# Batch 0 of an attention and MLP kernel: x by halves on two engines, the mean as one column, other fills for the matrix engine

## The chip, the cores and the metric

The kernel runs on one core of a Trainium2 chip. The metric is device time in microseconds (us). A core has a matrix engine (PE, whose weight loads are listed apart as PEld), a vector engine (DVE), a scalar engine for activations (ACT), a general one (POOL) and a queue engine for transfers (SP). Each takes its instructions in the order of the program and waits on semaphores that the others raise.

## The reference

For each of 8 batches and 8 heads, with 576 tokens of 64 dimensions, a linear attention is computed; its output, heads side by side, is a token's x of 512 numbers. Then a layer norm and an MLP with a residual follow:

```python
q_s = softmax(q, axis=-1)            # over the 64 dimensions of a head
k_s = softmax(k, axis=2)             # over the 576 tokens
kv  = einsum('bhsd,bhse->bhde', k_s, v)
x   = einsum('bhsd,bhde->bhse', q_s, kv)   # then (batch, token, 512)
xn  = (x - mean(x)) / sqrt(var(x) + 1e-6) * g_ln
out = x + maximum(xn @ w_ch1, 0) @ w_ch2   # 512 -> 2048 -> 512
```

## The kernel before, in words

Tokens are worked on in chunks: chunks 0 to 7 are the first 512 tokens of each batch, as 4 tiles of 128; chunk 8 gathers the remaining 64 tokens of each batch. For every chunk a list of MLP steps on PE (`mlp_steps`) is written out, and side work (the attention of a later chunk, weight sums, loads) is placed into it at given positions by `run`. Nothing is reordered: the schedule is manual, so the order of the calls is the order on each engine.

The change lies in the start, `first_batch`, and in what it calls. There all loads are issued, and batch 0 is brought to the point where its MLP can begin:

- `warm` issues matmuls on a tile of zeros (`junk`) that nothing reads; 17 stand at the start, 6 between the transposes of the first two token tiles.
- `exp_qt(0, t)` is the exponential of q for token tile t, on ACT; `norm_q` divides by the sum, on DVE; `eq_pT` transposes the result on PE (`ptr`) and copies it into `eqT`, on the engine named. Tiles 0 and 1 are normalized before the transpose, tiles 2 and 3 not.
- `exp_k0` and `z0_mm` give the exponential of k and its sums; `kv0_mm(j)` makes k'v for a pair of heads j in 6 matmuls, and one DVE instruction (line 322) scales it, keeps the two diagonal blocks and adds up each row (`kvbox["sum"]`). From this sum comes `mbc[:, j]`, a 128x128 tile in which each row holds minus the row's sum over 512. On ACT (line 327) for j = 0 to 2, on DVE (line 331) for j = 3.
- `xT_mm(j, kh)` builds x minus its mean for token tiles 0 and 1, already transposed, in PSUM (`pxT`): for each half kh of the 512 features one bank of two 128-blocks, with the kv product where the pair j belongs to the half, and with two products by `mbc[:, j]` that take the mean away. `xT_out(i)` evicts block i, times g, into `xnT`: blocks 0 and 1 on DVE (line 351), 2 and 3 on ACT (line 353).

Then `mlp_steps(0)` begins: four column blocks of w1 times the first feature half of tiles 0 and 1 (`ph`, line 520, w1 taken from `w1_raw`, whose first 512 columns come in two transfers, one for each half of the features). In between, at position 2 of `run`, z, po, x (`x_fast`, line 464) and xn (`x_normed`, line 475) of token tile 2; at 4 z and po of tile 3; then the second feature half; at 6 the transposes of tile 2's xn (`xn_pT`, line 928) and x of tile 3. The loads of v, q tiles 2 and 3, w1 and w2 are issued in this order by POOL, after a small copy (`gate`, line 1004) that waits for q tiles 0 and 1.

Of the kernel before, what the change touches and what calls it, by code (L numbers as in the profile page):

```python
# [12 lines left out]
FP32 = mybir.dt.float32  # L13
BF16 = mybir.dt.bfloat16
AF = mybir.ActivationFunctionType
# [5 lines left out]
def kernel(  # L21
# [16 lines left out]
    nc = tc.nc  # L38

    B, H, S, D = q.shape  # L40
    DM = H * D
    DH = 4 * DM
    P = 128
    T = 4
# [4 lines left out]
    NP = H // 2  # L49
# [10 lines left out]
    const = ctx.enter_context(tc.tile_pool(name="const", bufs=1))  # L60
# [12 lines left out]
    eps_ln = const.tile([P, 1], FP32)  # L73
    gate = const.tile([P, 4], FP32)
    ones = const.tile([P, 1], BF16)
    junk = const.tile([P, P], BF16)
    scrap = const.tile([P, 512], BF16)
    bones = const.tile([P, 2], BF16)
    ones_w = const.tile([P, P], BF16)
    diag = const.tile([P, P], FP32)  # L80
    mbc = const.tile([P, NP, P], BF16)
    g_one = const.tile([P, KO1], FP32)
    w1_sb = wts.tile([P, KO1, DH], BF16, name="w1_raw")
    w1g = const.tile([P, KO1, DH], BF16)
# [12 lines left out]
    def load_w1(nb):  # L97
        cols = slice(nb * 512, nb * 512 + 512)
        nc.gpsimd.dma_start(w1_sb[:, :, cols], w1_src[:, :, cols])
# [100 lines left out]
    def new_eq(c):  # L200
        eqs[c] = (
            att.tile([P, T, H, D], BF16, tag="eq", name="eq", bufs=1),
            sml.tile([P, T, H], FP32, tag="zq", name="zq"),
            sml.tile([P, T, H], FP32, tag="rq", name="rq"),
        )
        eqTs[c] = att.tile([P, T, NP, P], BF16, tag="eqT", name="eqT")
# [10 lines left out]
    def exp_qt(b, t):  # L217
        if t == 0 and b:
            new_eq(b)
        nc.scalar.activation(eqs[b][0][:, t], raws[b][2][:, :, t], AF.Exp)  # L220
# [66 lines left out]
    kvbox = {}  # L287
# [9 lines left out]
    def k0_mm(j, t):  # L297
        hs = slice(2 * j, 2 * j + 2)
        return eks[0][0:P0, t, hs, :], raws["v0"][0:P0, hs, t, :], P
# [16 lines left out]
    def kv0_mm(j):  # L316
        pool, tag = (att_ps, "a") if j < 2 else (mm_ps, "m")
        pkv = pool.tile([P, P], FP32, tag=tag, name="pkv")
        for t in range(T0):
            lhsT, rhs, w = k0_mm(j, t)  # L320
            nc.tensor.matmul(pkv[:, 0:w], lhsT, rhs, start=(t == 0), stop=(t == T0 - 1))
        nc.vector.scalar_tensor_tensor(
            kv_sb[:, 0, j, :], in0=pkv, scalar=kvbox["rz"][:, j : j + 1], in1=diag,
            op0=ALU.mult, op1=ALU.mult, accum_out=kvbox["sum"][:, j : j + 1],
        )
        if j < NP - 1:
            nc.scalar.activation(
                mbc[:, j], ones_w, AF.Copy, scale=kvbox["sum"][:, j : j + 1]
            )
        else:  # L330
            nc.vector.tensor_scalar_mul(
                out=mbc[:, j], in0=ones_w, scalar1=kvbox["sum"][:, j : j + 1]
            )

    def xT_mm(j, kh):

        if j == 0:
            pobox["T", kh] = mm_ps.tile([P, 2, 2, P], FP32, tag="m", name="pxT")
        ops = [(kv_sb[:, 0, j, :], j % 2)] if j // 2 == kh else []
        ops += [(mbc[:, j], i) for i in range(2)]  # L340
        for n, (lhsT, i) in enumerate(ops):
            nc.tensor.matmul(
                pobox["T", kh][:, i], lhsT, eqTs[0][:, 0:2, j, :],
                start=(j == 0 and n == 0), stop=(j == NP - 1 and n >= len(ops) - 2),
                skip_group_check=True,
            )

    def xT_out(i):
        dst, src = xnTs[0][:, 0:2, i, :], pobox["T", i // 2][:, i % 2]
        if i < 2:  # L350
            nc.vector.tensor_scalar_mul(out=dst, in0=src, scalar1=g_one[:, i : i + 1])
        else:
            nc.scalar.activation(dst, src, AF.Copy, scale=g_one[:, i : i + 1])
# [506 lines left out]
        for _, fn in side[done:]:  # L860
            fn()

    def warm(n):

        w = mm_ps.tile([P, 4, P], FP32, tag="m", name="warm")
        for _ in range(n):
            nc.tensor.matmul(w, junk, junk[:, 0:4].to_broadcast([P, 4, P]), start=True, stop=True)

    def prep_fast(b):

# [54 lines left out]
    def pe_T(dst, src, t, eng, scale=None):  # L925
        ptr = mm_ps.tile([P, NP, 2 * P], BF16, tag="m", name="ptr")
        for j in range(NP):
            nc.tensor.transpose(ptr[:, j, 0:P], src[:, j * P : j * P + P], ident)  # L928
        if eng is nc.scalar:
            nc.scalar.copy(dst[:, t], ptr[:, :, 0:P])  # L930
        elif scale is not None:
            nc.vector.tensor_mul(dst[:, t], ptr[:, :, 0:P], scale.to_broadcast([P, NP, P]))
        else:
            nc.vector.tensor_copy(out=dst[:, t], in_=ptr[:, :, 0:P])
# [10 lines left out]
    def eq_pT(c, t, eng):  # L945
        pe_T(eqTs[c], eqs[c][0][:, t].rearrange("p h d -> p (h d)"), t, eng)
# [10 lines left out]
    def first_batch():  # L957

        nc.scalar.preload_act_table_set("natural_log_exp_and_others")
        raws[0] = (  # L960
            mlp.tile([P, H, T0, D], FP32, tag="hT", name="kt0", bufs=1), None,
            raw.tile([P, H, T, D], FP32, tag="qt", name="qt"),
        )
        k0, _, q0 = raws[0]
        v0 = mlp.tile([P, H, T0, D], BF16, tag="hs", name="v0", bufs=1)
        raws["v0"] = v0

        def load_q0(t, tn, eng):
            ts = slice(t, t + tn)
            eng.dma_start(  # L970
                q0[:, :, ts],
                q[0, :, 0:SM, :].rearrange("h (p t) d -> p h t d", t=T)[:, :, ts],
            )

        def src0(x, h0, hn):
            return x[0, h0 : h0 + hn].rearrange("h (p t) d -> p h (t d)", t=T0)

        load_q0(0, 2, nc.sync)
        for h0 in range(0, H, 2):
            nc.sync.dma_start(  # L980
                k0[0:P0, h0 : h0 + 2].rearrange("p h t d -> p h (t d)"), src0(k, h0, 2)
            )
        raws["g"] = outp.tile([KO1, P], FP32, tag="ot", name="g_rows")
        nc.scalar.dma_start(
            raws["g"], bass.AP(moe_g_ln.tensor, moe_g_ln.offset, [[P, KO1], [1, P]])
        )
        nc.vector.memset(junk, 0.0)
        nc.vector.memset(eps_ln, 1e-6)
        nc.vector.memset(ones, 1.0)
        nc.vector.memset(bones, 0.0)  # L990
        nc.vector.memset(bones[0:64, 0:1], 1.0)
        nc.vector.memset(bones[64:P, 1:2], 1.0)
        nc.vector.memset(ones_w, -1.0 / DM)
        nc.vector.memset(diag, 0.0)
        for ps in halves:
            nc.vector.memset(diag[ps, ps], 1.0)
        nc.vector.memset(kv_sb[:, 1:B], 0.0)
        nc.vector.memset(vr, 0.0)
        for half in range(2):
            nc.vector.memset(vr[64 * half : 64 * half + 64, :, 4 * half : 4 * half + 4, D:], 1.0)  # L1000
        nc.vector.memset(vm[:, :, :, :, D:], 1.0)
        make_identity(nc, ident)
        nc.gpsimd.tensor_copy(out=ident_f, in_=ident[0:KO1, 0:KO1])
        nc.gpsimd.tensor_copy(out=gate, in_=q0[:, 1, 0, 0:4])
        for h0, hn in ((0, 4), (4, 2), (6, 2)):
            nc.gpsimd.dma_start(  # L1006
                v0[0:P0, h0 : h0 + hn].rearrange("p h t d -> p h (t d)"), src0(v, h0, hn)
            )
        for t in range(2, T):
            load_q0(t, 1, nc.gpsimd)  # L1010
        for kh in range(2):
            ks = slice(2 * kh, 2 * kh + 2)
            nc.gpsimd.dma_start(w1_sb[:, ks, 0:512], w1_src[:, ks, 0:512])
        for nb in range(1, 4):
            load_w1(nb)
        load_w2(0)
        load_w2(1)

        new_eq(0)
        start_x(0)  # L1020
        warm(17)
        for t in range(2):
            exp_qt(0, t)
            norm_q(0, t)
        eq_pT(0, 0, nc.vector)
        warm(6)
        eq_pT(0, 1, nc.vector)
        for j in range(NP):
            exp_k0(j)
            z0_mm(j)  # L1030
            if j == NP - 2:
                g_columns()
        recip_z()
        kv0_mm(0)
        kv0_mm(1)
        kv0_mm(2)
        xT_mm(0, 0)
        kv0_mm(3)
        exp_qt(0, 2)
        exp_qt(0, 3)  # L1040
        xT_mm(1, 0)
        xT_mm(2, 0)
        xT_mm(0, 1)
        xT_mm(3, 0)
        xT_out(0)
        xT_out(1)
        eq_pT(0, 2, nc.scalar)
        xT_mm(1, 1)
        xT_mm(2, 1)
        eq_pT(0, 3, nc.vector)  # L1050
        xT_mm(3, 1)
        xT_out(2)
        xT_out(3)

    def q0_rest(t):
        z_q(0, t)
        for i in range(NP):
            po_mm(0, t, i)
# [132 lines left out]
```

## Time and profile before

| what | value |
|---|---|
| time, median of 3 runs | 262.56 us (262.25 to 262.58) |
| the profiled execution | 262.09 us, span 260.3 us |
| PE busy | 98% of the span |
| DVE, ACT, POOL busy | 86%, 68%, 40% |
| transfers | 45.04 MB, 173 GB/s on the mean |
| PE idle for want of a w1 block, once, at 16.7 us | 0.4 us |

Times in the profile count from the start of the span. A line of the timeline gives the start and length of a group of instructions, its engine, line and operation, what it writes and reads, how many there are, and in brackets how long the engine had been idle before and which engine or transfer ended that. A matmul's length has its latency in it; how fast PE takes work is seen better from the distance of the weight loads.

### The profile page before, as it was taken

How to read it: one execution, taken by the hardware profiler on the slowest of the kernel's cores; microseconds unless marked ns; L12 is line 12 of the kernel's file. 1: busy time of each engine (PE TensorE's matmuls, PEld its weight loads, DVE VectorE, ACT ScalarE, POOL GpSimd, SP SyncE). 2: the span in 40 equal slices, each digit the busy share in tenths (PEclk: the TensorE clock that was granted, in tenths of full speed). 3: DMA queues.
4: the chain of work that ended last, by engine and by line, in shares of the span. 5: the costliest groups of instructions: out<-in, count | busy, mean ns of one | idle time of the engine just before them, and what ended most of it. 6: DMA issues, size and time to landing. Idle time of an engine off the chain costs nothing.

```text
span 260.3 us, 7286 instructions
## 1 busy us (share of the span) xinstructions
PE 253.9 (98%) x2885; PEld 215.6 (83%) x2885; DVE 223.1 (86%) x542; ACT 177.5 (68%) x348; POOL 103.2 (40%) x160
## 2 busy tenths in 40 slices
PE   8899999999999999999999999999999999999993
PEld 3689755788888888888888988888889888888883
DVE  6768996989989998899889988998899889957873
ACT  4747790997988685888588858885788386647400
POOL 3953247410299409800980098008200900190000
PEclk9999999999999999999999999999999999999999
DMA  6999999988699995999699859989902630422014
GB/s 198 257 203 208 354 221 332 257 169 308 118 122 321 268 120 107 300 247 107 142 300 235 86 135 304 232 89 161 279 0 50 142 137 1 77 71 99 3 40 121
DMA packets 82618, 45.04 MB, mean 173 GB/s; under 512 B 58196, under 2 KB 79192, under 8 KB 82584
## 3 DMA queue, kind: packets, MB, share of 16 engines
q0 software_dynamic: 32464, 21.76, 45.8%
q1 hardware_dynamic: 49488, 22.29, 36.8%
q10 hardware_dynamic: 632, 0.53, 0.7%
q8 instruction: 22, 0.36, 0.6%
q14 instruction: 12, 0.10, 0.1%
HBM read 36.70 MB, written 9.44 MB: 177 GB/s over the span
## 4 chain that ended last, share of the span: by engine, by line
PE 92%; DMA 4%; POOL 2%; DVE 0%; issue 0%
PE ba L604 21%; PE bx L762 20%; PE bb L762 10%; PE ph L520 8%; PE bb L604 6%; PE be L604 5%; PE bc L604 5%; PE pc L556 5%; PE bc L762 5%; DMA w_raw<-in_moe_w_ch_dram 3%; PE pkv L371 2%; DMA qt<-in_q_dram 2%; PE po L403 2%; PE ptr L928 1%; PE po L414 1%; POOL v L1006 1%
## 5 line engine op out<-in xcount | busy, mean ns | idle before, releaser
L604 PEld LDWEIGHTS <-hs 128*128 128x128 bf16 x512 | 49.6, 98 | 6.0
L269 POOL TENSOR_TENSOR tq<-xnT 128x256 bf16<-128x256 bf16 x30 | 20.1, 671 | 85.3 <-PE bc L604 73.9
L762 PEld LDWEIGHTS <-w_raw 128*128 128x128 bf16 x480 | 46.7, 98 | 5.5
L604 PEld LDWEIGHTS <-hT 128*128 128x128 bf16 x392 | 37.6, 98 | 4.2
L762 PEld LDWEIGHTS <-w1g 128*128 128x128 bf16 x360 | 34.7, 98 | 4.3 <-issue 0.2
L762 PE MATMUL bx<-tq,w_raw 128*128 128x256 bf16 x240 | 31.3, 273 | 0.0
L604 PE MATMUL ba<-w_q,hs 128*128 128x256 bf16 x256 | 30.6, 273 | 0.0
L786 ACT COPY bc<-bx 128x512 f32<-128x512 f32 x30 | 16.7, 596 | 19.1 <-PE bx L762 19.1
L427 ACT ACTIVATE scrap<-x,mv 128x512 bf16<-128x512 bf16 x32 | 23.1, 723 | 4.6 <-DVE mv L457 4.4
L793 DVE TENSOR_TENSOR bb<-bx,s 128x512 f32<-128x512 f32 x30 | 19.5, 694 | 7.2 <-ACT s L790 4.5
L804 ACT ACTIVATE hT<-bb 128x512 bf16<-128x512 f32 x30 | 16.3, 595 | 9.3 <-PE bb L762 9.3
L804 ACT ACTIVATE hT<-bc 128x512 bf16<-128x512 f32 x30 | 16.5, 595 | 8.5 <-PE bc L762 8.5
L796 DVE TENSOR_TENSOR hT<-bx,s 128x512 bf16<-128x512 f32 x30 | 19.3, 684 | 3.2 <-PE bx L762 3.1
L587 DVE TENSOR_TENSOR hs<-hT 128x1024 bf16<-128x1024 bf16 x32 | 21.4, 672 | 0.5 <-ACT hT L804 0.5
L229 DVE TENSOR_REDUCE zq<-eq 128x16 f32<-128x1024 bf16 (+1 forms) x20 | 20.7, 1049 | 0.5 <-ACT eq L220 0.5
L269 POOL TENSOR_TENSOR tq<-xnT,tq 128x256 bf16<-128x256 bf16 x30 | 20.0, 669 | 1.1
L449 DVE SCALAR_TENSOR_TENSOR x<-po,rq 128x256 bf16<-128x256 f32 x48 | 17.5, 420 | 1.7 <-PE po L403 1.7
L790 ACT COPY s<-bb 128x512 f32<-128x512 f32 x30 | 16.6, 622 | 0.0
L804 ACT ACTIVATE hT<-bx 128x512 bf16<-128x512 f32 x30 | 16.4, 610 | 0.0
L762 PE MATMUL bx<-xnT,w1g 128*128 128x256 bf16 x120 | 16.2, 273 | 0.0
L762 PE MATMUL bx<-tq,w1g 128*128 128x256 bf16 x120 | 15.9, 272 | 0.0
L762 PE MATMUL bc<-xnT,w1g 128*128 128x256 bf16 x120 | 15.8, 273 | 0.0
(157 smaller groups left out, 535.0 us busy)
## 6 DMA issues: line engine op xcount, KB each, us to landing
out_dram<-ot POOLq DMA_DIRECT2D x30, 256.0 KB, 4.4
kt<-in_k_dram SPq DMA_DIRECT2D x5, 1024.0 KB, 11.6
qt<-in_q_dram SPq DMA_DIRECT2D x4, 1024.0 KB, 9.9
qt<-in_q_dram POOLq DMA_DIRECT2D x2, 1024.0 KB, 12.7
kt<-in_k_dram POOLq DMA_DIRECT2D x2, 1024.0 KB, 14.5
vm<-in_v_dram POOLq DMA_DIRECT2D x16, 128.0 KB, 12.4
qt<-in_q_dram SPq DMA_DIRECT2D x3, 512.0 KB, 5.7
w_raw<-in_moe_w_ch_dram POOLq DMA_DIRECT2D x3, 512.0 KB, 10.5
```

The source lines that it names most:

```text
L229: nc.vector.reduce_sum(eqs[c][1][:, ts], eqs[c][0][:, ts], axis=AX.X)
L269: nc.gpsimd.tensor_tensor(out=dst[:, t], in0=x[:, t], in1=y[:, t], op=ALU.subtract)
L427: nc.scalar.activation(scrap, x[:, t], AF.Square, bias=mv[:, t, 0:1], scale=-float(DM), accum_out=mv[:, t, 1:2],)
L449: nc.vector.scalar_tensor_tensor(x[:, t].rearrange("p (i two d) -> p i two d", two=2, d=D)[:, :, half], in0=pobox[c, t][half], scalar=1.0, ...
L520: nc.tensor.matmul(ph[:, m % 2, at : at + tn], (w1g if c else w1_sb)[:, ko, m * P : (m + 1) * P], xnTs[c][:, t0 : t0 + tn, ko, :], start=( ...
L587: nc.vector.tensor_tensor(out=dst, in0=x, in1=y, op=op)
L604: nc.tensor.matmul(hbox[bank][:, t, cs], lhsT, rhs[:, cs], start=first and (own or t == 0) and k == 0, stop=k == KH - 1, skip_group_check= ...
L762: nc.tensor.matmul(dst[:, q], lhsT, rhs, start=first and q == 0 and ko == 0, stop=ko == 1, skip_group_check=True)
L786: nc.scalar.copy(at[g, "c"], at[g, "x"])
L793: nc.vector.tensor_tensor(out=at[g, "b"], in0=at[g, "x"], in1=at[g, "s"], op=ALU.add)
L796: nc.vector.tensor_tensor(out=h_out(g, 1, 1), in0=at[g, "x"], in1=at[g, "s"], op=ALU.add)
L804: nc.scalar.activation(h_out(g, odd, half), at[g, name], AF.Relu)
```

## The change

Four things change, all in the start of batch 0.

1. `mbc` and the tile of constants `ones_w` go. In their place is `kvm`, one column for each pair j: the row's sum times -1/512. `xT_mm` gives the matrix engine this column as a 128x128 weight tile, read 128 times with step 0.
2. `xT_out`: blocks 0 and 2 go to DVE, 1 and 3 to ACT.
3. The order. Before, the products of x with the second half stood between those of the first, and the transposes of token tiles 2 and 3 among them, the copy of tile 2 on ACT and of tile 3 on DVE; both `exp_qt(0, 2)` and `exp_qt(0, 3)` stood ahead of them. Now the first half is finished and evicted, then comes `exp_qt(0, 3)`, the second half and its eviction, and then the transposes of tiles 2 and 3, with both copies on DVE. As before, `xT_mm(0, 0)` stands ahead of the last kv product.
4. The fills: `junk` is a float32 tile, with a bf16 one (`junk_h`) beside it. In place of 17 bf16 fills there are 4 float32 ones, in place of 6 there are one float32 and two bf16.

```diff
-    junk = const.tile([P, P], BF16)
+    junk = const.tile([P, P], FP32)
+    junk_h = const.tile([P, P], BF16)
-    ones_w = const.tile([P, P], BF16)
-    mbc = const.tile([P, NP, P], BF16)
+    kvm = const.tile([P, NP], BF16)
...
+        total = kvbox["sum"][:, j : j + 1]
         if j < NP - 1:
-            nc.scalar.activation(
-                mbc[:, j], ones_w, AF.Copy, scale=kvbox["sum"][:, j : j + 1]
-            )
+            nc.scalar.activation(kvm[:, j : j + 1], total, AF.Copy, scale=-1.0 / DM)
         else:
-            nc.vector.tensor_scalar_mul(
-                out=mbc[:, j], in0=ones_w, scalar1=kvbox["sum"][:, j : j + 1]
-            )
+            nc.vector.tensor_scalar_mul(out=kvm[:, j : j + 1], in0=total, scalar1=-1.0 / DM)
...
-        ops += [(mbc[:, j], i) for i in range(2)]
+        ops += [(kvm[:, j : j + 1].to_broadcast([P, P]), i) for i in range(2)]
...
-        if i < 2:
+        if i % 2 == 0:
             nc.vector.tensor_scalar_mul(out=dst, in0=src, scalar1=g_one[:, i : i + 1])
...
-    def warm(n):
+    def warm(n, src=junk):
...
-            nc.tensor.matmul(w, junk, junk[:, 0:4].to_broadcast([P, 4, P]), start=True, stop=True)
+            nc.tensor.matmul(w, src, src[:, 0:4].to_broadcast([P, 4, P]), start=True, stop=True)
...
         nc.vector.memset(junk, 0.0)
+        nc.vector.memset(junk_h, 0.0)
...
-        nc.vector.memset(ones_w, -1.0 / DM)
...
-        warm(17)
+        warm(4)
...
-        warm(6)
+        warm(1)
+        warm(2, junk_h)
...
-        kv0_mm(0)
-        kv0_mm(1)
-        kv0_mm(2)
+        for j in range(NP - 1):
+            kv0_mm(j)
         xT_mm(0, 0)
-        kv0_mm(3)
+        kv0_mm(NP - 1)
         exp_qt(0, 2)
-        exp_qt(0, 3)
-        xT_mm(1, 0)
-        xT_mm(2, 0)
-        xT_mm(0, 1)
-        xT_mm(3, 0)
+        for j in range(1, NP):
+            xT_mm(j, 0)
         xT_out(0)
         xT_out(1)
-        eq_pT(0, 2, nc.scalar)
-        xT_mm(1, 1)
-        xT_mm(2, 1)
-        eq_pT(0, 3, nc.vector)
-        xT_mm(3, 1)
+        exp_qt(0, 3)
+        for j in range(NP):
+            xT_mm(j, 1)
         xT_out(2)
         xT_out(3)
+        for t in range(2, T):
+            eq_pT(0, t, nc.vector)
```

## The prediction

> **What bounds the kernel now.** I read four views, from the whole to the place of the change. First the page's engine line, which says that the matrix engine is the bound on average:
>
> ```profile
> PE 253.9 (98%) x2885; PEld 215.6 (83%) x2885; DVE 223.1 (86%) x542; ACT 177.5 (68%) x348; POOL 103.2 (40%) x160
> ```
>
> Then the chain that ended last, in order of time (start, length, what):
>
> ```profile
> 0.74 4.29 DMA qt<-in_q_dram
> ...
> 9.82 6.86 DMA w_raw<-in_moe_w_ch_dram
> 16.68 0.05 issue
> 16.72 0.61 PE ph L520 x4
> ...
> 19.74 11.37 PE ph L520 x112
> 31.11 2.37 PE pc L556 x11
> ```
>
> Up to 16.72 us the chain is transfers: q, the descriptors behind it on POOL, then the second 256 KB block of w1. From 16.72 on it is PE without a hole. So what the change does ahead of 16.72 counts only where it makes PE or its feeders miss that point; behind it, a delay goes one to one to the end. The waits of PE over the whole run say the same, for besides the first instruction there are only these:
>
> ```profile
> PE ptr L928 <- DVE eq L923: 1.0, 1, 1.0
> PE ph L520 <- DMA w_raw<-in_moe_w_ch_dram: 0.4, 1, 0.4
> ```
>
> Last the timeline of the place itself (start, length, engine, line, in brackets the idle time before):
>
> ```profile
> 11.14 1.17 ACT L327 ACTIVATE mbc<-ones_w,kvs 128x128 bf16<-128x128 bf16 x3 [1.16 <-DVE kv_sb L322]
> ...
> 12.44 1.40 ACT L220 ACTIVATE eq<-qt 128x512 bf16<-128x512 f32 x2
> ...
> 12.77 0.25 DVE L331 TENSOR_SCALAR mbc<-ones_w,kvs 128x128 bf16<-128x128 bf16 x1
> 13.07 0.11 PEld L342 LDWEIGHTS <-mbc 128*128 128x128 bf16 x2 [0.26 <-DVE mbc L331]
> ...
> 13.51 0.88 DVE L351 TENSOR_SCALAR xnT<-pxT,g_one 128x256 bf16<-128x256 f32 x2 [0.49 <-PE pxT L342]
> ...
> 14.52 0.42 PEld L520 LDWEIGHTS <-w_raw 128*128 128x128 bf16 x4
> ...
> 15.90 0.23 PEld L414 LDWEIGHTS <-eqT 128*128 128x128 bf16 x4
> ...
> 16.40 0.35 DVE L475 TENSOR_SCALAR xn<-x,st 128x512 bf16<-128x512 bf16 x1
> ...
> 16.72 0.33 PEld L520 LDWEIGHTS <-w_raw 128*128 128x128 bf16 x4 [0.59 <-DMA w_raw<-in_moe_w_ch_dram]
> ...
> 17.06 0.32 PEld L928 LDWEIGHTS <-xn 128*128 128x128 bf16 x4
> ```
>
> The reader is to see two slacks. The last weight load ahead of the w1 wait ends at 16.13, so PE's queue could run 0.59 us later for nothing. The transpose of xn for token tile 2 is loaded at 17.06, and its source is done at 16.40 + 0.35 = 16.75; with the 0.05 us from a DVE end to a load (13.02 to 13.07) that chain has 0.26 us.
>
> **The change, part by part.** The profiled execution took 262.09 us (span 260.3, 1.8 around it), 0.47 under the median of the runs, 262.56. I add differences in the profile to the median.
>
> *Fills.* PE now begins with 4 float32 fills for 17 bf16 ones, and has 1 float32 and 2 bf16 for 6.
>
> ```profile
> 3.96 0.15 PEld L867 LDWEIGHTS <-junk 128*128 128x128 bf16 x1 [0.28 <-issue]
> ...
> 4.31 1.62 PEld L867 LDWEIGHTS <-junk 128*128 128x128 bf16 x8 [0.20 <-issue]
> ...
> 9.73 0.29 PEld L953 LDWEIGHTS gcp<-ident_f,g_rows 4*128 4x128 f32 x2
> ```
>
> The loads come every 0.43 us up to 3.96 and every 0.21 us after 4.31: PE runs at half pace for its first 3.3 us. The one float32 product shows as two loads and two matmuls, so a float32 fill costs at least two bf16 fills, and at most four if the doubled bytes also halve the pace of each; I take four, the dearer. [...] From 1.05 (the float32 memset is 0.165 as for diag, 0.112 before) two fills take 1.71 each and two 0.85 each: they end near 6.2, where the 17 ended at 6.42. PE then waits for DVE's normalized eq until 7.41 in both. The second group is 0.85 + 2 x 0.21 = 1.28 against 6 x 0.21 = 1.28, plus a float32 load of 0.18 in place of 0.10: 0.07 later at the second transpose. On DVE the memsets add 0.05 + 0.11 and remove 0.165 (ones_w): nothing.
>
> *Mean as one column.* Four 128x128 writes become 128x1. ACT: three of 0.40 become 0.21 (nearest row the 128x4 rstd at 0.206; bounds 0.08, DVE's accumulator read of one column, and 0.40, no gain). DVE: 0.254 becomes 0.14 (row L1124, 128x1; bounds 0.08 and 0.254). The first column is ready 0.19 earlier, so the last kv product could start at 11.64 in place of 11.83. But the third v block was issued at 6.7 and lands 5.0 later, at 11.7; I take 11.75. So the fourth kv step on DVE starts at 12.29 (12.37), its column is ready at 12.83 (13.02), and x's bank is complete for eviction at 13.32 (13.51): 0.19 gained. That 0.08 of gain at the v block also swallows the 0.07 of the fills. The 16 weight loads now read a column with step 0; mbc's take 98 ns at a pitch of 107. The fills read their moving side with step 0 at full pace, so I take 98; the dear bound is 182, the float32 load.
>
> *The evictions.* xT_out(1) goes from DVE to ACT. In the compiled order of the changed kernel that ACT instruction waits for a DVE semaphore which xT_out(0) sets; both read one PSUM tile. So they run one behind the other: DVE 13.32 to 13.80 (0.478), ACT 13.83 to 14.30 (0.470), against 14.39 before: 0.09 gained, not 0.4. [...]
>
> *What is queued behind that wait.* On ACT it is exp_qt(0, 3), which ran from 13.21 to 13.84. It now starts at 14.20 (two such ACT evictions had a pitch of 0.37, 14.83 to 15.67 for two) and ends at 14.83. PE holds its order: the transposes of token tile 3 now stand ahead of x's first products with w1, and both wait. Transposes at 14.88, and 0.27 later (13.97 to 14.24 before) the first w1 load at 15.15, against 14.52: 0.63 later, although x itself was ready earlier. The transposes of tile 2 and the other half of x (ten matmuls at 0.107) fit into the hole at 13.1 to 14.88. The two eqT copies, both on DVE now (0.42 each), end near 15.8, ahead of z for tile 3 near 16.3. xT_out(3) on ACT, behind the late exp, ends near 15.3; the products of the second half stand near 16.7. Both are covered, by 0.5 and 1.4 us. SP and POOL issue the same transfers in the same order, so w1 lands when it did.
>
> *Sum.* PE reaches the w1 wait at 16.13 + 0.63 = 16.76: only 0.04 over. But z, po, x_fast and xn of tile 2 also move by 0.63, so xn ends at 17.38 and its transposes load at 17.43 against 17.06: **0.37 us later**. From there the DVE and PE steps to tile 3 (19.34) are a tight chain, and PE is dense to the end. Forecast: 262.56 + 0.37 = 262.93, say **262.95 us**, slower by a breath. Its own range: without the v wait and with the short columns 0.17 less, 262.75; with columns as dear as before (0.08 + 0.11), no overlap on ACT (0.10) and the fills' 0.07 uncovered, 263.3.
>
> **The rivals.**
>
> *1. The fills leave PE at half pace* (slower). Place: the load pitch at 4 us. If 4 float32 fills do not lift the pace at 4.3, they last to 1.05 + 4 x 1.71 = 7.9, past 7.41: 0.5 later at the first transposes, which all passes on, since DVE, ACT and PE to xn of tile 2 form one chain; with 0.37 that is 263.4. If the pace stays low to the w1 wait, some 3 us of PE work (24 products of 0.06, 20 of 0.107) doubles besides: about 265. It decides once half pace lasts past 6. For it: a third of the fills' instructions, and 1.2 us idle behind them. Against: by the dearer price PE is busy as long as before. [...]
>
> *2. The one-column loads are slow* (slower). At 182 ns each of 16 loads costs 0.075 more than the pitch: 0.6 ahead of xT_out(0), with 0.1 covered by the wait for the fourth column: 262.95 + 0.5 = 263.5. Against: step 0 runs at full pace on the moving side.
>
> *3. The delay is swallowed, or the two evictions do overlap* (not slower). If ACT's eviction ran from 13.32, exp_qt(0, 3) would end at 14.32 and the first w1 load come at 14.64: 0.12 late, under both slacks, so 262.56. It decides where exp_qt(0, 3) ends before 14.45. Against: the semaphore.
>
> *4. Faster.* The w1 landing is not moved, and in before nothing between 16.72 and the end waits for anything the change touches. Only what no row shows (other PSUM banks and SBUF addresses, a different phase of the pace) could give it: 262.0.
>
> **How the numbers follow.** A difference of 0.2%, 0.53 us, is about what a measurement of this kernel can tell from none. Forecast 0.57; of its own range a good third lies past 263.08, so 0.22 slower and 0.35 same. Rival 1: 0.15 and rival 2: 0.08, slower. Rival 3: 0.10, same. Rival 4: 0.10, faster. Together: faster 0.10, same 0.45, slower 0.45. The range leaves out half of rival 4 and the dear half of rival 1: 262.3 to 264.2.
>
> **What would show it.** In the profile of the changed kernel: xT_out(1) on ACT starting after xT_out(0) on DVE has ended; exp_qt(0, 3) behind it, ending near 14.8; a new wait of PE transposes on ACT of some 0.5 us; the w1 wait nearly gone; the transposes of xn for tile 2 near 17.4. Right on the fills: loads or matmuls at full pace by 4.5. I am wrong if PE still waits 0.4 us for w1, if the step-0 loads take over 0.11, or if fills run into 7.4.

## The result, and the profile after

| what | value |
|---|---|
| kernel before, median of 6 runs beside the changed one | 262.49 us (262.0 to 262.76) |
| changed kernel, median of 6 runs | 263.84 us (263.69 to 264.9) |
| ratio, with its 95% interval | 1.0061 (1.0042 to 1.0081) |
| profiled execution of the changed kernel | 264.3 us, span 262.5 us |

The change makes the kernel 1.35 us slower. I had forecast a loss of 0.37 us. The profiled execution lies 0.46 us above the median, so its details are read with that in mind. From here on "before" and "after" are the two kernels, and a kernel that I made is called by what it changes.

The page of after has PE still nearly full, with eleven fewer instructions:

```profile
PE 255.6 (97%) x2874; PEld 215.8 (82%) x2874; DVE 223.8 (85%) x543; ACT 176.3 (67%) x347; POOL 103.3 (39%) x160
```

The waits of PE in after, besides its first instruction (engine, tile and line, what it waited for: us in total, times, longest):

```profile
PE z L306 <- ACT ek L293: 0.5, 1, 0.5
PE ptr L925 <- DVE eq L920: 0.4, 1, 0.4
PE bb L759 <- DVE hT L526: 0.4, 1, 0.4
PE ptr L925 <- ACT eq L220: 0.3, 1, 0.3
```

The wait for w1 is gone, as forecast, and the transposes of tile 3 wait for ACT's exponential, as forecast. But the first line is new and lies, in time, ahead of all that the new order touches: PE waits for the last exponential of k. The chain that ended last, from its beginning (start, length, what), leads to the same place:

```profile
2.85 7.33 DMA kt<-in_k_dram
10.18 0.02 issue
10.20 0.85 ACT ek L293
11.06 0.05 issue
11.10 0.30 PE z L306 x6
```

In before the chain began with q and went through w1, and k stood nowhere in it. The timeline of after shows how the delay travels (start, length, engine and line, what; in brackets the idle time before):

```profile
5.41 1.15 ACT L220 ACTIVATE eq<-qt 128x512 bf16<-128x512 f32 x2 [3.39 <-DMA qt<-in_q_dram]
...
10.20 0.84 ACT L293 ACTIVATE ek<-kt 96x768 bf16<-96x768 f32 x1 [0.30 <-DMA kt<-in_k_dram]
...
14.37 0.48 DVE L348 TENSOR_SCALAR xnT<-pxT,g_one 128x256 bf16<-128x256 f32 x1 [0.49 <-PE pxT L339]
...
14.88 0.47 ACT L350 ACTIVATE xnT<-pxT,g_one 128x256 bf16<-128x256 f32 x1 [0.32 <-DVE xnT L348]
...
15.26 0.62 ACT L220 ACTIVATE eq<-qt 128x512 bf16<-128x512 f32 x1
...
16.11 0.37 PEld L517 LDWEIGHTS <-w_raw 128*128 128x128 bf16 x4
...
18.42 0.23 PEld L925 LDWEIGHTS <-xn 128*128 128x128 bf16 x4 [0.41 <-DVE xn L472]
```

The point on which the forecast turned, the transposes of xn for tile 2, comes at 18.42 in place of 17.06: 1.36 us later, which is the loss of the medians. But xT_out(0) already starts at 14.37 in place of 13.51, although each step that the change touches ahead of it became shorter or stayed. So 0.86 of the 1.36 is there before the new order has done anything. (In this execution another 0.8 us is lost behind 18.42, in two waits, near 34.8 and 58.8 us; of the kernels below with late transfers some have both, some only the first and one has neither, and I draw nothing from them.)

What is late is transfers. The answer on transfers for the first 12 us, before (bytes and mean rate; for the queue q1 its packets, their MB and the time they took as a share of what the 16 DMA engines have; then for each kind of transfer its size and the median us from issue to landing):

```profile
DMA packets 2816, 2.73 MB, mean 227 GB/s; under 512 B 147, under 2 KB 2711, under 8 KB 2816
...
q1 hardware_dynamic: 1872, 1.70, 50.6%
...
kt<-in_k_dram SPq DMA_DIRECT2D x4, 288.0 KB, 5.5
...
qt<-in_q_dram POOLq DMA_DIRECT2D x2, 256.0 KB, 5.0
w_raw<-in_moe_w_ch_dram POOLq DMA_DIRECT2D x2, 256.0 KB, 6.1
```

and the same of after:

```profile
DMA packets 2719, 2.42 MB, mean 201 GB/s; under 512 B 130, under 2 KB 2689, under 8 KB 2719
...
q1 hardware_dynamic: 1872, 1.70, 58.4%
...
kt<-in_k_dram SPq DMA_DIRECT2D x4, 288.0 KB, 6.3
...
qt<-in_q_dram POOLq DMA_DIRECT2D x2, 256.0 KB, 6.3
w_raw<-in_moe_w_ch_dram POOLq DMA_DIRECT2D x2, 256.0 KB, 6.7
```

The same transfers, of the same size, in the same order on the same queues, move 11% less in the same time. They are not cut into more packets: the queue q1 moves 1872 packets with 1.70 MB both times, and these packets take longer, 58.4% of the engines' time in place of 50.6%. The edit to the calls cannot do that: it touches no transfer. So the experiments had two questions: which part of the change slows transfers that it does not name, and what is left of the loss once they run as before.

### The profile page after: what moved, and what is told of

Its sections match the earlier page's. It is cut to its first block, busy times and chain, and to the rows that moved or that the text cites. A ratio compares the mean times of both kernels' runs of the same rounds, so it can differ in the third digit from the quotient of the medians.

```text
span 262.5 us, 7264 instructions
## 1 busy us (share of the span) xinstructions
PE 255.6 (97%) x2874; PEld 215.8 (82%) x2874; DVE 223.8 (85%) x543; ACT 176.3 (67%) x347; POOL 103.3 (39%) x160
## 4 chain that ended last, share of the span: by engine, by line
PE 77%; DMA 15%; POOL 2%; DVE 2%; issue 1%; SPq 1%; ACT 1%; POOLq 0%
PE ba L601 21%; PE bx L759 20%; PE bb L759 10%; DMA w_sb<-in_moe_w_ch_dram 8%; PE bb L601 6%; PE be L601 5%; PE bc L601 5%; PE bc L759 5%; DMA vr<-in_v_dram 4%; DMA kt<-in_k_dram 3%; PE pkv L368 2%; PE po L400 2%; PE pxT L339 1%; POOL kt L130 1%; DVE w_q L567 1%
## 5 line engine op out<-in xcount | busy, mean ns | idle before, releaser
L759 PE MATMUL bb<-tq,w_raw 128*128 128x256 bf16 x120 | 15.7, 272 | 0.4 <-DVE hT L526 0.4
```

Of the source, the lines that this page charges most:

```text
L759: nc.tensor.matmul(dst[:, q], lhsT, rhs, start=first and q == 0 and ko == 0, stop=ko == 1, skip_group_check=True)
```

## The experiments

Every kernel here computes the whole result, and each ratio is to the kernel before, run beside it on the same chip (262.30 us in the first group of runs, 262.29 in the second, 262.58 in the third, whose chip gave wider intervals).

**First group: the parts, one by one.** The column alone: `mbc` and `ones_w` out, `kvm` in, with the old fills, evictions and order of calls.

```diff
-    ones_w = const.tile([P, P], BF16)
     diag = const.tile([P, P], FP32)
-    mbc = const.tile([P, NP, P], BF16)
+    kvm = const.tile([P, NP], BF16)
...
-        ops += [(mbc[:, j], i) for i in range(2)]
+        ops += [(kvm[:, j : j + 1].to_broadcast([P, P]), i) for i in range(2)]
```

> Before with the mean as one column and nothing else. Step-0 weight loads at full pace: 98 ns each at a pitch of 107 ns, x's first bank complete 0.1 to 0.2 us earlier, the time the same as before to 0.2 us, since the w1 wait takes up the gain. Slow loads would show as 0.15 us and more each, and 0.3 us or more on the time.

Measured: 263.58 us, ratio 1.0052 (1.0035 to 1.0069). A part that saves work on ACT and DVE brings nearly the whole loss. The timeline of this kernel shows where:

```profile
10.51 0.84 ACT L292 ACTIVATE ek<-kt 96x768 bf16<-96x768 f32 x1 [0.40 <-DMA kt<-in_k_dram]
...
15.32 0.63 ACT L219 ACTIVATE eq<-qt 128x512 bf16<-128x512 f32 x1 [0.46 <-DMA qt<-in_q_dram]
```

The last exponential of k starts at 10.51, against 9.1 in before, and that of q tile 3 waits for its transfer until 15.32, though in this kernel it still stands ahead of the evictions. Both waits end with a transfer.

The column with the new fills added:

```diff
-    junk = const.tile([P, P], BF16)
+    junk = const.tile([P, P], FP32)
+    junk_h = const.tile([P, P], BF16)
...
-        warm(17)
+        warm(4)
...
-        warm(6)
+        warm(1)
+        warm(2, junk_h)
```

> The old order and the old evictions, with the one-column mean and the float32 fills. If the time is lost to the order (exp_qt(0, 3) and the transposes of tile 3 late), this is within 0.3 us of before. If it is lost to the fills (half pace held to about 6.5 us, or q and k landing later beside them), it is slower by most of the 1.35 us that the full change lost, that is by 0.8 us or more, and its profile shows k's last block on ACT near 10 us and not near 9.1.

Measured: 263.72 us, 1.005 (1.0033 to 1.0068): 0.14 us over the column alone, well inside both intervals. The fills are not where the time went. (The new fills were not tried on before alone.)

The whole change with the old fills:

```diff
-        warm(4)
+        warm(17)
...
-        warm(1)
-        warm(2, junk_h)
+        warm(6)
```

> The full change but with the 17 and 6 bf16 fills. If the order loses the time, it stays slower than before by 0.4 to 1.35 us. If the fills lose it, it is within 0.4 us of before. Pace: loads of the fills every 0.21 us from about 4.3 us on, as in before.

Measured: 263.24 us, 1.0041 (1.0024 to 1.0058). The interval overlaps that of after, and q tiles 2 and 3 are late here too (5.9 us to landing). The two pairs put the new fills at 0.14 us and at 0.41 (1.35 less 0.94), neither of it clear of the intervals.

The new order of calls alone, on before (the block from `kv0_mm` on, as in the change; evictions and `mbc` as before):

```diff
-        exp_qt(0, 3)
-        xT_mm(1, 0)
-        xT_mm(2, 0)
-        xT_mm(0, 1)
-        xT_mm(3, 0)
+        for j in range(1, NP):
+            xT_mm(j, 0)
         xT_out(0)
         xT_out(1)
-        eq_pT(0, 2, nc.scalar)
...
+        exp_qt(0, 3)
...
+        for t in range(2, T):
+            eq_pT(0, t, nc.vector)
```

> Before with the new order of calls and nothing else (old fills, mbc, both first evictions on DVE). exp_qt(0, 3) then waits behind nothing on ACT but exp_qt(0, 2), so the transposes of tile 3 stand only behind x's second half: if the late exp behind the eviction is the loss, this is within 0.2 us of before; if the transposes standing ahead of the first w1 products are the loss by themselves, it is slower by 0.3 us or more.

Measured: 262.72 us, 1.0011 (1.0 to 1.0022), 0.42 us in the medians; the interval begins at nothing. Transfers land as in before (q tiles 2 and 3 in 5.2 us). So the order costs about what I had given it. But it did not lose it in the way I had described, as this kernel's chain shows:

```profile
12.81 0.69 DVE mbc L331
13.50 0.05 issue
13.55 1.48 PE pxT L342 x12
15.03 0.24 PE ptr L928 x4
15.27 0.03 issue
15.29 0.76 DVE eqT L934 x2
```

With both evictions on DVE, `exp_qt(0, 3)` isn't late here: it ends at 13.88, against 13.84 before. What is late is the column on DVE (0.69 long in place of 0.25), and with it xT_out(0), by 0.47 us. The transposes of xn for tile 2 are late by 0.46, no more:

```profile
13.98 0.88 DVE L351 TENSOR_SCALAR xnT<-pxT,g_one 128x256 bf16<-128x256 f32 x2 [0.49 <-PE pxT L342]
...
17.52 0.23 PEld L928 LDWEIGHTS <-xn 128*128 128x128 bf16 x4 [0.34 <-DVE xn L475]
```

From the one to the other it takes 3.54 us, as in before (3.55, from 13.51 to 17.06), where 0.26 of it was slack. So the new order has a second price, near 0.25 us: the transposes stand behind the second half of x, and their two copies, both on DVE now, stand ahead of the reciprocal that x of tile 2 needs. In this execution that price went into the slack, and the longer column alone accounts for the loss. Why the column took longer isn't known, so the 0.42 us can't be put down to the new queueing.

**Second group: addresses.** What the column part changes for a transfer is where its target lies. In the compiled programs the tiles of SBUF follow each other. `mbc` and `ones_w` take 1280 bytes of each partition, `kvm` 8, for which 32 are set aside; so every tile behind it moves by 1248 bytes. In before the tiles of q, k and the first w1 start at multiples of 256 bytes. With the column alone, and in after, they start 32 bytes past such a multiple. The theory: this is the cause, and neither the step-0 loads nor the column itself. The plainest test takes before, changes no instruction of the work and adds a tile that nothing reads (with a memset of one element):

```diff
     mbc = const.tile([P, NP, P], BF16)
+    pad = const.tile([P, 16], BF16)
...
+        nc.vector.memset(pad[0:1, 0:1], 0.0)
```

> Before with one unused tile of 32 bytes per partition behind mbc, and no other change in what is computed or in which order. If the start address is the cause, 1.0 to 1.4 us slower than before, with q landing near 5.4 and k's last block after 9.9 us. If not, within 0.2 us of before.

Measured: 263.61 us, 1.0062 (1.0039 to 1.0085). Thirty-two bytes that nobody uses cost 1.32 us, as much as the whole change. Its transfers in the first 12 us and its chain:

```profile
DMA packets 2719, 2.41 MB, mean 201 GB/s; under 512 B 130, under 2 KB 2691, under 8 KB 2719
...
qt<-in_q_dram POOLq DMA_DIRECT2D x2, 256.0 KB, 6.3
w_raw<-in_moe_w_ch_dram POOLq DMA_DIRECT2D x2, 256.0 KB, 6.7
```

```profile
8.52 6.37 DMA qt<-in_q_dram
14.89 0.02 issue
14.91 0.64 ACT eq L221
15.55 0.05 issue
15.60 0.40 PE ptr L929 x4
```

These are after's figures, 201 GB/s, 6.3 and 6.7, out of a program that has before's work to the instruction. The unused tile moves the operands of the engines as well as the targets of transfers. But the first transfer of q, issued at 0.74 us, when no engine works on these tiles yet, already takes 4.6 us here, in place of the 4.3 in before, so the transfers themselves are slower.

The counter-test keeps the column and gives its tile 256 bytes, so that all behind it starts at multiples of 256 again:

```diff
-    kvm = const.tile([P, NP], BF16)
+    kvm = const.tile([P, P], BF16)
```

> As the run before, padded to 256 bytes, so that the targets keep before's address modulo 256 as well. If a multiple of 64 is enough, it is as fast as with 64 bytes; if 256 counts, this one is at 262.3 and the one with 64 bytes is slower by 0.4 us or more.

Measured: 262.26 us, 1.0001 (0.9989 to 1.0014). The loss of the column is gone to the last tenth, and its transfers are before's:

```profile
DMA packets 2813, 2.71 MB, mean 226 GB/s; under 512 B 147, under 2 KB 2711, under 8 KB 2813
...
qt<-in_q_dram POOLq DMA_DIRECT2D x2, 256.0 KB, 5.0
```

The same with 64 bytes (`const.tile([P, 32], BF16)`):

> Before with the one-column mean alone, but the column's tile padded from 8 to 64 bytes per partition, so that q, k, v and w1 start at a multiple of 64 bytes again as in before; nothing else differs from the run with the column alone, which lost 1.28 us. If the loss is the start address of the transfers' targets, this is within 0.3 us of before and k's last block reaches ACT near 9.2 us. If the column itself loses it (the weight loads, the missing memset), it stays at 263.3 or more and k's last block comes after 10 us.

Measured: 263.43 us, 1.0044 (1.0031 to 1.0057), q tiles 6.2 us to landing. A start at a multiple of 64 is not enough.

The whole change with its column tile at 256 bytes, the same one-line edit:

> The full change with the column's tile padded to 256 bytes. If the address explains all but the order, what is left is the late exp_qt(0, 3) behind the eviction on DVE, by the prediction 0.37 us: 262.5 to 262.9. If address and order do not add up, as slow as the full change, 263.6 or more.

Measured: 262.63 us, 1.0015 (1.0006 to 1.0024). This is the forecast's own case, with the transfers as in before: +0.34 us against the forecast's 0.37. Its chain through the place:

```profile
13.61 0.50 DVE xnT L348
14.11 0.02 issue
14.13 0.47 ACT xnT L350
14.61 0.53 ACT eq L220
15.13 0.05 issue
15.18 0.40 PE ptr L925 x4
...
17.19 0.37 DVE xn L472
17.55 0.05 issue
17.60 0.40 PE ptr L925 x4
```

**Third group: what is left.** The last 0.34 us: the late exponential, or the rest of the order? The whole change with aligned tiles, and `exp_qt(0, 3)` back ahead of the evictions:

```diff
+        exp_qt(0, 3)
         xT_out(0)
         xT_out(1)
-        exp_qt(0, 3)
```

> The full change with the column's tile padded to 256 bytes, and exp_qt(0, 3) moved ahead of xT_out(0). If the exponential queued behind the eviction on ACT is what the change itself costs, this is back at 262.3, within 0.15 us of before, with the transposes of tile 3 loaded before 14.6 us. If the transposes standing ahead of the first w1 products are enough by themselves, it stays at 262.6 or so, as with the padding alone.

Measured: 262.77 us, 0.9998 (0.9978 to 1.0018). The interval holds both nothing and the 0.34 us, so the time settles nothing. In the trace the exponential is early, ending at 13.29, and from xT_out(0) to the transposes of xn it takes 3.72 us (13.11 to 16.83), where the kernel just above took 3.99 and before 3.55. Of before's 3.55 us 0.26 was slack. Some of the price goes with the exponential, some stays, as far as one execution of each can show it.

The whole change with aligned tiles and the old order of calls:

```diff
+        exp_qt(0, 3)
+        xT_mm(1, 0)
+        xT_mm(2, 0)
+        xT_mm(0, 1)
+        xT_mm(3, 0)
...
+        eq_pT(0, 2, nc.scalar)
...
```

> All of the change but the new order of calls, padded to 256 bytes: one-column mean, evictions of each half on DVE and ACT, float32 fills. If only the order costs anything once the addresses are as in before, 262.3, within 0.15 us of before. If the fills or the evictions cost something beside it, 262.5 or more.

Measured: 262.36 us, 0.9992 (0.9963 to 1.0021), and 3.30 us for that stage. Column, split evictions and new fills together lose nothing that can be told from before, and gain nothing either.

The column alone with a tile of 128 bytes (`const.tile([P, 64], BF16)`):

> Before with the column alone, its tile padded to 128 bytes: q, k, v and w1 start at a multiple of 128 and not of 256 bytes. If 256 is what counts, as slow as with 64 bytes, 263.2 to 263.6; if 128 is enough, 262.3.

Measured: 263.13 us, 1.0029 (1.0006 to 1.0051), q tiles 5.9 us. A multiple of 128 doesn't do either, by the time and by the q tiles. The loss in the medians, 0.55 us, is smaller, and k takes 5.8 us to landing here (median), next to the 5.1 to 6.0 of the seven kernels with aligned tiles. Whether 128 is milder than 32 isn't settled: the five kernels at 32 past a multiple of 256 gave 5.9 to 6.5 us for the q tiles, and the intervals of the times overlap.

The column at 256 bytes, and small tiles and two unused ones made wide enough that the targets of w2 and of the later v tiles start at multiples of 256 as well (in before w2's starts 96 bytes past one):

```diff
-    g_one = const.tile([P, KO1], FP32)
+    g_one_w = const.tile([P, 64], FP32)
+    g_one = g_one_w[:, 0:KO1]
...
+    pad_a = const.tile([P, 112], BF16)
     vm = const.tile([P, 2, T, H, VW], BF16)
+    pad_b = const.tile([P, 64], BF16)
```

> Before with the column padded to 256 bytes, and with small pads that also bring w2, the rest tiles of v and the v tiles of later batches to a multiple of 256 bytes. If a start off 256 bytes slows any transfer into SBUF, the w2 loads land earlier than in before; the time moves little, since PE waits for no transfer after 16.7 us: 262.0 to 262.3. A time above 262.5 would speak against the address as the cause.

Measured: 262.46 us, 0.9993 (0.9972 to 1.0013), and w2 lands in 16.0 us as in before. Nothing is to be had there: no version beat before by more than its interval.

## Why the prediction was right or wrong

Sign and range were right, the place and most of the size were not. The forecast was 262.95 us, the result 263.84; of the loss of 1.35 us the forecast had 0.37. That the result lies inside the range is luck: the upper part of the range stood for slow fills and slow column loads (rivals 1 and 2), and neither of them cost time.

*The step that failed* is the sentence that closes the part on the queued work: "SP and POOL issue the same transfers in the same order, so w1 lands when it did." The first half is true, and the second doesn't follow. The loads of the first 15 us land later, since their targets moved by an amount that isn't a multiple of 256 bytes. Among those are k, whose last exponential starts at 10.20 in place of 9.1, and q tiles 2 and 3. I had the thought in the wrong rival: SBUF addresses stand under "Faster", as something "no row shows", with 0.10. They belonged on both sides, and the addresses could have been read from the compiled program without a run. Shown by: before with 32 unused bytes has the loss, the column with 256 bytes has none.

For 256 stand the q tiles 2 and 3 of the four kernels that differ in the column's tile alone: 6.5, 6.2 and 5.9 us to landing with 32, 64 and 128 bytes set aside for it, 5.0 with 256. By what mechanism the start of the written side slows a transfer no run shows.

*The step that held* is the sum for the order: 0.37 us forecast, 0.34 with aligned tiles (262.63 against 262.29, ratio 1.0015, 1.0006 to 1.0024, that is 0.16 to 0.63 us). In that kernel the second eviction starts on ACT 0.02 after the first has ended on DVE (14.13 after 14.11), so they aren't side by side, and rival 3 falls. In after, too, the second eviction's wait (0.32 us on ACT, until 14.88) is ended by the first; what two side by side would do no run shows. The exponential starts behind it, the transposes load 0.05 behind its end. The points I had named, 13.32, 13.83, 14.20, 14.88 and 17.43, came at 13.61, 14.13, 14.51, 15.18 and 17.60, the first four about 0.3 late, because k's last exponential started 0.4 later in that execution (9.49), the last 0.17 late. In this trace the transposes of xn come 0.54 later than in before, so that 0.34 lies so near to 0.37 is in part luck. The cause was only half right: the two copies on DVE and the transposes behind x's second half, which I had called covered, have a price of their own. From xT_out(0) to the transposes of xn it takes 3.72 us with the new order and the exponential early, against 3.30 with the old order. How the 0.34 splits between the two stays open; early exponential and old order both gave intervals that hold it.

*The two losses do not add in the medians.* Addresses alone cost 1.32 us, the order alone 0.34 to 0.42, both together 1.35. The interval of the whole change, 1.1 to 2.1 us, holds their sum too, so the times don't settle it. In the kernel with 32 unused bytes the exponential of q tile 3 waits for its transfer until 14.91, so that most of the time by which the order delays it in after (to 15.26) has gone already: the transposes of xn come at 18.34 there and at 18.42 in after. That is argued from the two traces, not shown by the times.

*The column* is as forecast. In the kernel with the column at 256 bytes (durations in ns min/median/max, first and last start):

```profile
L338 PEld LDWEIGHTS <-kvm x16: 95/98/100, 11.4 to 14.2; 128*128 128x128 bf16 x16
L327 ACT ACTIVATE kvm<-kvs x3: 205/205/206, 11.1 to 11.9; 128x1 bf16<-128x1 f32 x3
L329 DVE TENSOR_SCALAR kvm<-kvs x1: 156/156/156, 12.7 to 12.7; 128x1 bf16<-128x1 f32 x1
```

I took 98 ns for the load with step 0, 0.21 us on ACT and 0.14 on DVE. Rival 2 falls. The 0.19 us that it was to bring shows in no time: 1.0001 (0.9989 to 1.0014).

*The fills* ran as in the dearer price: a float32 fill shows as two records, 0.85 us apart at half pace (loads at 2.07, 2.92 and 3.77 in after), so 1.7 together, what four bf16 fills take at before's 0.43. Rival 1's condition came true, its consequence did not. Half pace lasted past 6 us in after and in the aligned kernels with the new fills (to 6.4 and beyond), but PE waits behind it all the same, in after for DVE until 7.77. From the first transposes to the second it is 1.56 us in before (7.41 to 8.97) and in after (7.77 to 9.33): not even the 0.07 I had charged. In the kernel with the early exponential, where k came early, the chain does run through the fills, but its last z still loads at 9.95, against 10.04 in before. The pace does not rise at one time: in five executions with bf16 fills the first load at the higher pace comes at 4.3, 3.9, 4.4, 4.8 and 5.6 us, and in the kernel with the column and the new fills the pace rises already between 3.8 and 4.3. What sets that time no run shows.

*The wait for w1* vanished as forecast (0.4 us of wait gone), because PE arrives late: its first load of w1 comes at 16.11 in place of 14.52. But PE had to arrive later for it than I had in mind, since w1 itself took 0.6 us longer to land (6.7 for 6.1).

## What to carry to other kernels

When a tile is removed, added or resized in a pool that packs its tiles, look first at what lies behind it: compare the start addresses of the transfer targets in the two compiled programs, and if they lose a multiple of 256 bytes, which cost 0.55 to 1.32 us of 262 here, pad the tile before anything else is judged. When a part of the profile that the diff does not touch has changed, as the landing times did here, put that part to the test alone, by a kernel that has only the suspected side effect. And an edit that moves an instruction behind another engine's wait costs what its last consumer loses, but only as long as nothing else makes that consumer later still: with late transfers the transposes of xn came at 18.34 without the new order and at 18.42 with it, in one execution of each.

## What the runs showed of the hardware

- In the start of this kernel, transfers into SBUF are slower where their targets don't start at multiples of 256 bytes. Over fourteen kernels the 256 KB tiles of q took 4.9 to 5.3 us from issue to landing in the seven with such starts, and 5.9 to 6.5 in the seven with starts 32, 64 or 128 past one, with no overlap; from before to after the rate over the first 12 us fell from 227 to 201 GB/s. The packets are the same (1872 in q1) and take longer (58.4% of the engines' time for 50.6). On this kernel of 262 us it cost 1.1 to 1.3 us with starts 32 or 64 past a multiple, 0.55 with 128; with 32 unused bytes the transposes of xn for tile 2 are already 1.28 late (18.34 for 17.06), so nearly all of that is lost in the start. Which of the transfers must be aligned wasn't tested apart. For w2, whose transfers are issued behind those of w1 (from 12.73 on, after 10.53, in before), the start made no difference: 16.0 us in before, with starts 96 past a multiple, and 16.0 in the kernel with all of them aligned.
- The stores of the result, 30 of 256 KB, moved in SBUF with the rest. They took 4.2 to 4.5 us to landing (medians) in the seven kernels with aligned tiles and 4.6 to 5.6 in the other seven; what that costs wasn't measured.
- A weight load that reads one column 128 times with step 0 takes 98 ns (95 to 100 over 16 loads, in the kernel with the column at 256 bytes), as long as a load of 128 columns of `mbc` in before (98, 95 to 100).
- The same 128x128 write on DVE took 0.25 us in before and 0.69 in the kernel with the new order alone, each in one execution. Why isn't known.
